# One accumulator bank per block product, and a scale vector spread by the matrix engine, in a fused attention and feed-forward kernel

## The chip, the core and the metric

The kernel runs on one core of a Trainium2 chip. A core has a matrix engine (TensorE, PE in the profile, with its weight loads listed as PEld), VectorE (DVE), ScalarE (ACT), GpSimd (POOL), a sync engine that here only issues transfers (SP), and 16 DMA engines. The engines run their own instruction streams and meet at semaphores. Matrix products land in PSUM, an accumulator memory made of banks; one tile of the pool `mm` below is one bank (128 partitions x 512 fp32). VectorE and ScalarE read PSUM and write the results back to SBUF.

The metric is the device time of one execution in microseconds (us), the median of several runs. The profile of one execution shows a span that is about 2 us shorter than that time.

## The reference

A chunked attention is followed by a feed-forward block with a residual.

```python
# q, k, v: (4, 8, 768, 64); mem_k, mem_v: (4, 8, 8, 64)
for c in range(24):                                   # chunks of 32 queries
    k_full = concat(mem_k, k[c*32-16 : c*32+40])      # 8 memory rows, 16 to the left, 8 to the right
    v_full = concat(mem_v, v[same])
    a = softmax(q_c @ k_full.T / sqrt(64))
    out[c] = a @ v_full
x  = out as (4, 768, 512)
mu, var = mean(x), mean((x - mu)**2)                  # over the last axis
xn = (x - mu) / sqrt(var + 1e-6) * g_ln               # g_ln: 512 numbers
y  = x + max(xn @ w_ch1, 0) @ w_ch2                   # 512 -> 2048 -> 512
```

## The kernel before

The rows are worked in 24 tiles of 128, three tiles to a stage, eight stages (`u` = 0 to 7). A stage has 28 steps: 16 steps of the first product (`up`, line 411), then the second product (`down`, line 441). From stage 2 on, two of the three tiles of the second product are computed together as a 2x2 block product with seven block multiplications in place of eight (a Winograd form): the left sums are `SA`, the right sums `T`, and each of the seven is a `product` (line 484) of eight matmuls of 128x256. They stand in steps 20 to 26, after `down` of the third tile.

```python
def product(p, left, right):                          # line 484
    for h in range(2):
        for k_ in range(4):
            nc.tensor.matmul(out=p, lhsT=left(h)[:, k_, :], rhs=right(h)[:, k_, :], ...)

def paired(u, n):                                     # n = 0 .. 6
    cols = [slice(0, 256), slice(256, 512)]
    # scaled(r, y, z, w): osb[r][:, w] = y * rstd[r] + z[r][:, w]   on VectorE (line 500)
    # minus(o, a, b, op): o = a op b                                on VectorE (line 458)
    for m in {0: (0,), 2: (2,), 3: (4, 3)}.get(n, ()):
        pair_slot[m] = slot("mm")                     # next of the four mm banks
    q = pair_slot
    if n == 0:
        product(q[0][:, cols[0]], a(0, 0), b(0, 0))
        nc.scalar.copy(out=three[:, 0, :], in_=q[0][:, cols[0]])       # line 524
    elif n == 1:
        product(q[0][:, cols[1]], part(SA, 1), part(T, 1))             # same bank as n == 0
        minus(psum, q[0][:, cols[1]], three[:, 0, :], ALU.add)
    elif n == 2:
        product(q[2][:, cols[0]], part(SA, 0), part(T, 0))
        minus(three[:, 2, :], q[2][:, cols[0]], psum, ALU.add)
        for h in range(2):
            mixed_r(h, 3)                             # the left sum that product 5 needs
        scaled(0, free(three, 0, [[512, 2], [1, 256]]), x)
    elif n == 3:
        product(q[3][:, cols[1]], part(SA, 2), part(T, 2))
        minus(three[:, 1, :], q[3][:, cols[1]], psum, ALU.add)
        scaled(1, free(three, 256, [[1, 512]]), x)
        if u == 7:
            scaled(1, q[3][:, cols[1]], o, cols[1])
            store(1, cols[1])
    elif n == 4:
        product(q[4][:, cols[0]], a(0, 1), b(1, 0))
    elif n == 5:
        product(q[4][:, cols[1]], part(SA, 1), b(1, 1))
        scaled(0, q[4], o)
        store(0)
    else:                                             # n == 6
        product(q[3][:, cols[0]], a(1, 1), part(T, 3))
        w = cols[0] if u == 7 else slice(0, 512)
        scaled(1, q[3][:, w], o, w)
        store(1, w)
```

The values of the eight memory rows are copied into the value buffers `V` by `v_mem`, 12 groups to a batch. For batches 2 and 3 ScalarE does this, in three copies of 8x2560 that the schedule puts in stages 1 and 3:

```python
for i in range(3):
    at(w - 1, (16, 19, 21)[i], v_mem, b, 4 * i, 4 * i + 4, act)   # w - 1 is stage 1, then stage 3
```

Ahead of the stages stands a start in which every step waits for its first data. The vector g_ln is read from memory 128 times, once for each partition, into `gb`, and used by `norm`. `warm(n)` are matmuls on zeros whose results nobody reads; they keep the matrix engine occupied.

```python
first_load(0, 0, 0, 32, nc.sync)                      # k of the first block
first_load(0, 1, 0, 32, nc.scalar)
nc.sync.dma_start(out=memkf, in_=...)                 # mem_k
first_load(1, 0, 0, 16, nc.sync)                      # q of the first block, in halves
first_load(1, 1, 0, 16, nc.gpsimd)
first_load(1, 0, 16, 32, nc.sync)
first_load(1, 1, 16, 32, nc.sync)
nc.sync.dma_start(out=xs[5][96:W, :], in_=...)        # mem_v of batch 0
nc.sync.dma_start(out=gb, in_=dram(moe_g_ln, 0, [[0, 128], [1, 512]]))
...                                                   # GpSimd queue: k, then V groups 0 and 1, w1, V 2 and 3, q, w1, ...
def norm(b, t):                                       # line 357
    i = NT * b + t
    nc.vector.scalar_tensor_tensor(
        out=xn[i % 4], in0=xs[i % 9], scalar=nmean[t], in1=gb, op0=ALU.add, op1=ALU.mult)
...
K0 = [as16(mm[0]), as16(mm[1])]
Q0 = [as16(mm[2]), as16(mm[3])]
...
scores(0, 0)
mem_vals()                                            # ScalarE: mem_v to fp16
soften(0, 0, 0)
soften(0, 0, 1)
mix(0, 1, 0, dve)
transpose_block(0, 1, 0, Q0)
v_mem(0, 0, 2, dve)
mix_raw(1, raws[1], None, dve, 64, 128)               # second half of q
warm(2, 512, att[1][:, 0, :])
half_q(0, 0, 1, as16(att[1][:, 1, :]))
first_right(0, 3, Q0)
part_q(0, 0, 1, as16(att[1][:, 1, :]), dve)
v_mem(0, 2, 4, dve)
values(0, 0)                                          # line 337: needs V groups 0 and 1
norm(0, 0)
window(0, 0, K0, 2, act)
window(0, 0, K0, 3, act)
warm(2, 512, att[0][:, 1, :])
scores(0, 1)
soften(0, 1, 0)
soften(0, 1, 1)
warm(4, 512, mm[1])
turn_x(0, 0)
values(0, 1)                                          # V groups 2 and 3
norm(0, 1)
...
late = up_tile(0, 0, 0, None)                         # first tile of stage 0; needs w1
```

Of the kernel before, what the change touches and what calls it, by code (L numbers as in the profile page):

```python
# [11 lines left out]
ALU = mybir.AluOpType  # L12
# [3 lines left out]
def kernel(  # L16
# [12 lines left out]
    nc = tc.nc  # L29
# [60 lines left out]
    def dram(t, offset, pattern):  # L90
        return bass.AP(tensor=t.tensor, offset=offset, ap=[list(p) for p in pattern])

    def free(ap, off, pattern, parts=None):
        p = list(ap.ap[0]) if parts is None else [ap.ap[0][0], parts]
        return bass.AP(tensor=ap.tensor, offset=ap.offset + off, ap=[p] + [list(x) for x in pattern])

    def as16(t):
        return t.bitcast(FP16)
# [104 lines left out]
    def first_right(b, g, banks):  # L203

        for half in range(2):
            copy(dve, free(KT[b % 2], GW * g + 80 + 4 * half, [[W, 4], [1, 4]]),
                 free(banks[half], 0, [[1, 4], [128, 4]]))
# [11 lines left out]
    def transpose_block(b, blk, which, banks):  # L219
        i = pick(iv, ("b", b, blk, which))  # L220
        for r in range(8):
            pv = banks[r // 4 if len(banks) == 2 else 0]
            c = 128 * (r % 4 if len(banks) == 2 else r)
            nc.tensor.matmul(  # L224
                out=pv[:, c : c + 128], lhsT=i[:, 128 * r : 128 * r + 128], rhs=identity,
                is_transpose=True, start=True, stop=True,
            )
# [26 lines left out]
    def part_q(b, blk, half, pv, eng):  # L254
        copy(eng, free(QR[b % 2], 1024 * blk + 64 * half, [[128, 8], [1, 64]]),
             free(pv, 64 * half, [[128, 8], [1, 64]]))

    def mix_raw(which, srcs, half, eng, lo=0, hi=128):

        o = pick(iv, ("b", 0, 0, which))[lo:hi, :]  # L260
        r0, n = (0, 8) if half is None else (4 * half, 4)
        for par in range(2):
            copy(eng, free(o, 128 * r0 + 64 * par, [[128, n], [1, 64]]),
                 free(srcs[par][lo:hi, :], 64 * r0, [[64, n], [1, 64]]))
# [87 lines left out]
            out=nmean[t], in0=tot[t], scalar1=-1.0 / 512, scalar2=None, op0=ALU.mult  # L352
        )

    def norm(b, t):
        i = NT * b + t
        nc.vector.scalar_tensor_tensor(  # L357
            out=xn[i % 4], in0=xs[i % 9], scalar=nmean[t], in1=gb, op0=ALU.add, op1=ALU.mult,
        )
# [97 lines left out]
    def minus(o, x, y, op=ALU.subtract):  # L457
        nc.vector.tensor_tensor(out=o, in0=x, in1=y, op=op)  # L458
# [22 lines left out]
    def product(p, left, right):  # L481
        for h in range(2):
            for k_ in range(4):
                nc.tensor.matmul(  # L484
                    out=p, lhsT=left(h)[:, k_, :], rhs=right(h)[:, k_, :],
                    start=(h == 0 and k_ == 0), stop=(h == 1 and k_ == 3),
                )
# [3 lines left out]
    def paired(u, n):  # L491

        t = 3 * u
        o = [osb[(t + r) % 3] for r in range(2)]
        x = [xs[(t + r) % 9] for r in range(2)]
        rs = [rstd[(t + r) % 9] for r in range(2)]
        cols = [slice(0, 256), slice(256, 512)]

        def scaled(r, y, z, w=slice(0, 512)):
            nc.vector.scalar_tensor_tensor(  # L500
                out=o[r][:, w], in0=y, scalar=rs[r], in1=z[r][:, w], op0=ALU.mult, op1=ALU.add,
            )

        def store(r, w=slice(0, 512)):
            i = t + r
            nc.sync.dma_start(
                out=out[i // 6, 128 * (i % 6) : 128 * (i % 6) + 128, w], in_=o[r][:, w]
            )

        def b(c, d):  # L510
            return lambda h: w2c[2 * c + h][:, :, cols[d]]

        def a(r, c):
            return lambda h: quarter(r, c, h)

        def part(lst, m):
            return lambda h: lst[m][h]

        for m in {0: (0,), 2: (2,), 3: (4, 3)}.get(n, ()):
            pair_slot[m] = slot("mm")  # L520
        q = pair_slot
        if n == 0:
            product(q[0][:, cols[0]], a(0, 0), b(0, 0))
            nc.scalar.copy(out=three[:, 0, :], in_=q[0][:, cols[0]])  # L524
        elif n == 1:
            product(q[0][:, cols[1]], part(SA, 1), part(T, 1))
            minus(psum, q[0][:, cols[1]], three[:, 0, :], ALU.add)
        elif n == 2:
            product(q[2][:, cols[0]], part(SA, 0), part(T, 0))
            minus(three[:, 2, :], q[2][:, cols[0]], psum, ALU.add)  # L530
            for h in range(2):
                mixed_r(h, 3)
            scaled(0, free(three, 0, [[512, 2], [1, 256]]), x)
        elif n == 3:
            product(q[3][:, cols[1]], part(SA, 2), part(T, 2))
            minus(three[:, 1, :], q[3][:, cols[1]], psum, ALU.add)
            scaled(1, free(three, 256, [[1, 512]]), x)
            if u == 7:
                scaled(1, q[3][:, cols[1]], o, cols[1])
                store(1, cols[1])  # L540
        elif n == 4:
            product(q[4][:, cols[0]], a(0, 1), b(1, 0))
        elif n == 5:
# [3 lines that stand above are left out]
        else:  # L547
# [5 lines that stand above are left out]
    def warm(n, m=512, p=None):  # L553
        p = mm[3] if p is None else p
        for _ in range(n):
            nc.tensor.matmul(out=p[:, 0:m], lhsT=zero[:, 0:128], rhs=zero[:, 0:m], start=True, stop=True)
# [4 lines left out]
    def first_load(which, par, lo, hi, eng):  # L561
        eng.dma_start(
            out=raws[which][par][4 * lo : 4 * hi, :],
            in_=dram((k, q)[which], 4 * par * HS + 512 * lo, [[512, hi - lo], [HS, 4], [1, 512]]),
        )
# [3 lines left out]
    nc.sync.dma_start(out=memkf, in_=dram(mem_k, 0, [[512, 32], [1, 512]]))  # L569
    first_load(1, 0, 0, 16, nc.sync)  # L570
    first_load(1, 1, 0, 16, nc.gpsimd)
    first_load(1, 0, 16, 32, nc.sync)
    first_load(1, 1, 16, 32, nc.sync)
    nc.sync.dma_start(out=xs[5][96:W, :], in_=dram(mem_v, 0, [[64, 8], [512, 8], [1, 64]]))
    nc.sync.dma_start(out=gb, in_=dram(moe_g_ln, 0, [[0, 128], [1, 512]]))

    def load_mem_v():
        nc.gpsimd.dma_start(
# [28 lines left out]
    nc.vector.memset(zero, 0.0)  # L607
    clear_keys(0, dve)
    nc.vector.memset(mhalf, -0.5)
    nc.vector.memset(memv16.bitcast(FP32)[96:W, :, :, 32:40], PAIR)  # L610
    total(band[:, 0:1], 56, 96)
    total(band[:, 1:2], 0, 32)
# [36 lines left out]

    K0 = [as16(mm[0]), as16(mm[1])]  # L650
    Q0 = [as16(mm[2]), as16(mm[3])]
    warm(10)
    mix_raw(0, raws[0], 0, dve)
    mix_raw(0, raws[0], 1, act)
# [15 lines left out]
    soften(0, 0, 0)  # L670
    soften(0, 0, 1)
    mix(0, 1, 0, dve)
    transpose_block(0, 1, 0, Q0)
    v_mem(0, 0, 2, dve)
    mix_raw(1, raws[1], None, dve, 64, 128)
    warm(2, 512, att[1][:, 0, :])
    half_q(0, 0, 1, as16(att[1][:, 1, :]))
    first_right(0, 3, Q0)
    part_q(0, 0, 1, as16(att[1][:, 1, :]), dve)
    v_mem(0, 2, 4, dve)  # L680
    values(0, 0)
    norm(0, 0)
    window(0, 0, K0, 2, act)
    window(0, 0, K0, 3, act)
    warm(2, 512, att[0][:, 1, :])
    scores(0, 1)
    soften(0, 1, 0)
    soften(0, 1, 1)
# [1 line left out]
    turn_x(0, 0)  # L690
    values(0, 1)
    norm(0, 1)
    window(0, 1, Q0, 0, act)
    window(0, 1, Q0, 1, act)
    key_left(0, 4, dve)
    turn["mm"] = 3
    late = up_tile(0, 0, 0, None)
# [2 lines left out]
    Q1 = as16(slot("mm"))  # L700
    half_q(0, 1, 0, Q1)
    part_q(0, 1, 0, Q1, act)
    window(0, 1, Q0, 2, dve)
    window(0, 1, Q0, 3, act)
    turn_x(0, 1)
    scores(0, 2)
    soften(0, 2, 0)
# [96 lines left out]
    for b in (2, 3):  # L804
        u = 2 * b - 1
        w = u - 1
        for blk in range(3):
            if b == 3 and blk == 0:
                at(w - 1, 0, pace, 0, 0)
            at(w - 1, 0 if b == 3 else 21, load_pair, b, blk)  # L810
        at(w, 0, mem_cols, b, pool)
        at(w - 1, 24, pace_x, 6 * b - 4)
        for g in range(NG):
            at(w - 1, 24 + g // 4, load_v, b, g)
        for i in range(3):
            at(w - 1, (16, 19, 21)[i], v_mem, b, 4 * i, 4 * i + 4, act)
        for blk in range(3):
            for which in range(2):
                at(w, (3, 9, 18)[blk] + which, mix, b, blk, which, dve)
                at(w, (7, 18, 23)[blk] + 3 * which, cross, b, blk, which)  # L820
        at(w, 18, spread, b, 0, dve, act)
        at(w, 27, spread, b, 1, dve, act)
        at(u, 9, spread, b, 2, dve, act)
        attend(6 * b, 2, 7, u)
        attend(6 * b + 1, 7, 13, u)
        attend(6 * b + 2, 13, 18, u)
# [61 lines left out]
```

## Time and profile before

| | |
|---|---|
| time, median of 3 runs | 223.66 us (223.60 to 223.71) |
| span of the profiled run | 221.6 us |
| PE busy | 209.3 us, 2116 matmuls |
| VectorE, ScalarE, GpSimd busy | 156.8, 124.7, 101.3 us |
| line 411 (`up`), 448 matmuls of 128x384 | 78.5 us |
| line 441 (`down`), 192 of 128x512 | 45.0 us |
| line 484 (`product`), 336 of 128x256 | six groups of 56 |
| ScalarE copies of memory values into V, 6 of 8x2560 | 13.8 us, 2320 ns each |

How to read it: the page gives for each engine its busy time, then the span in 40 slices of 5.54 us with the busy share in tenths, the granted clock of the matrix engine and what the DMA engines did. The chain of work that ended last follows the end of the span back to what released each step. The timeline gives each engine's instructions in order of time, with the idle time before them in brackets and who ended it. A letter q after an engine's name is its queue.

### The profile page before, as it was taken

The numbers are of one execution on the slowest core, as the hardware profiler recorded it, in microseconds if no ns is written. First come the engines' busy times: TensorE is split into PE (matmuls) and PEld (weight loads), VectorE is DVE, ScalarE is ACT, GpSimd is POOL, SyncE is SP. The second block draws the span as 40 slices with busy tenths as digits, with TensorE's granted clock in tenths as the row PEclk, the third lists the DMA queues.
The fourth block names the chain that finished last, engine by engine and source line by source line (L and its number), as shares of the span: only waits on it lengthen the run. The fifth ranks groups of instructions, "written<-read, shape, count | busy, mean of one in ns | idle before, by whom it ended". The sixth has DMA issues, their size and how long they took to land.

```text
span 221.6 us, 5419 instructions
## 1 busy us (share of the span) xinstructions
PE 209.3 (94%) x2116; PEld 142.7 (64%) x2116; DVE 156.8 (71%) x396; ACT 124.7 (56%) x242; POOL 101.3 (46%) x173
## 2 busy tenths in 40 slices
PE   7779999999999999999997999999999999999992
PEld 2437996557655566587655776586757675676571
DVE  5747467597969967985686678983888469563564
ACT  3735678418789768435899467427841576024100
POOL 7857589798998992407531983200111011100000
PEclk9967999999999999999999999999999999999999
DMA  6999999999979999697972999496312211220012
GB/s 167 172 194 191 199 198 188 196 148 241 161 103 152 184 194 120 110 189 159 196 121 74 91 186 130 96 165 144 26 24 71 98 24 28 71 95 3 0 47 95
DMA packets 72449, 27.98 MB, mean 126 GB/s; under 512 B 60392, under 2 KB 68328, under 8 KB 72424
## 3 DMA queue, kind: packets, MB, share of 16 engines
q0 software_dynamic: 46112, 14.71, 62.4%
q1 hardware_dynamic: 26168, 12.67, 27.2%
q10 hardware_dynamic: 144, 0.26, 0.5%
q8 instruction: 16, 0.26, 0.5%
q14 instruction: 9, 0.07, 0.1%
HBM read 30.54 MB, written 6.29 MB: 166 GB/s over the span
## 4 chain that ended last, share of the span: by engine, by line
PE 74%; ACT 4%; DVE 2%; issue 1%; ACTq 0%
PE mm L411 34%; PE mm L441 16%; PE mm L484 16%; PE att L316 5%; PE att L337 3%; ACT V L102 2%; DVE osb L500 1%; ACT three L524 1%; PE att L224 1%; PE mm L224 1%; ACT junk L362 0%; ACT AT L326 0%; PE att L385 0%; DVE SA L458 0%; DVE three L458 0%
## 5 line engine op out<-in xcount | busy, mean ns | idle before, releaser
L411 PE MATMUL mm<-xT,w1c 128*128 128x384 f16 x448 | 78.5, 328 | 0.0
L411 PEld LDWEIGHTS <-w1c 128*128 128x128 f16 x448 | 49.1, 114 | 21.0
L403 ACT ACTIVATE rT<-mm 128x384 f16<-128x384 f32 (+1 forms) x76 | 37.9, 502 | 37.5 <-PE mm L411 33.2
L405 DVE TENSOR_SCALAR rT<-mm 128x384 f16<-128x384 f32 (+1 forms) x48 | 27.3, 568 | 26.1 <-PE mm L411 25.6
L441 PE MATMUL mm<-w2c,rT 128*128 128x512 f16 x192 | 45.0, 380 | 0.0
L128 POOL DMA_DIRECT2D V<-in_v_dram x48 | 37.8, 795 | 6.8 <-DMA V<-in_v_dram 2.9
L326 ACT ACTIVATE AT<-att,band 104x512 f16<-104x512 f32 x48 | 31.3, 685 | 12.4 <-PE att L316 11.9
L368 POOL TENSOR_SCALAR veps<-sq 128x1 f32<-128x1 f32 x24 | 7.6, 318 | 64.3 <-ACT junk L362 56.2
L441 PEld LDWEIGHTS <-rT 128*128 128x128 f16 x192 | 17.7, 98 | 18.7
L484 PEld LDWEIGHTS <-SA 128*128 128x128 f16 x192 | 18.8, 98 | 6.9 <-issue 4.8
L362 ACT ACTIVATE junk<-xs,nmean 128x512 f16<-128x512 f32 x24 | 17.4, 725 | 9.1 <-DVE nmean L351 6.9
L484 PE MATMUL mm<-T,SA 128*128 128x256 f16 x144 | 16.7, 272 | 3.7 <-ACT three L524 3.7
L357 DVE SCALAR_TENSOR_TENSOR xn<-xs,nmean,gb 128x512 f16<-128x512 f32 x24 | 17.9, 747 | 0.3
L345 DVE SCALAR_TENSOR_TENSOR xs<-att,rec 128x512 f32<-128x512 f32 x24 | 16.6, 692 | 0.8
L372 POOL TENSOR_TENSOR rstd<-veps,mhalf 128x1 f32<-128x1 f32 x24 | 15.8, 658 | 2.0
L484 PEld LDWEIGHTS <-rT 128*128 128x128 f16 x144 | 14.1, 98 | 4.0 <-issue 1.0
L316 PE MATMUL att<-QR,KT 64*104 64x64 f16 x384 | 15.8, 234 | 0.7 <-ACT QR L102 0.6
L316 PEld LDWEIGHTS <-KT 64*104 64x104 f16 x384 | 12.6, 132 | 5.3 <-issue 3.7
L120 POOL DMA_DIRECT2D st<-in_k_dram x22 | 13.8, 662 | 1.8 <-DMA w1c<-in_moe_w_ch_dram 1.4
L337 PEld LDWEIGHTS <-AT 104*64 104x64 f16 x384 | 8.5, 114 | 8.5 <-issue 2.9
L102 ACT COPY V<-memv 8x2560 f16<-8x2560 f16 x6 | 13.8, 2320 | 0.1
L120 POOL DMA_DIRECT2D st<-in_q_dram x20 | 12.1, 650 | 1.2 <-DMA w2c<-in_moe_w_ch_dram 0.5
(92 smaller groups left out, 252.3 us busy)
## 6 DMA issues: line engine op xcount, KB each, us to landing
out_dram<-osb SPq DMA_DIRECT2D x23, 256.0 KB, 2.2
V<-in_v_dram POOLq DMA_DIRECT2D x40, 96.0 KB, 6.1
st<-in_k_dram POOLq DMA_DIRECT2D x22, 128.0 KB, 5.9
st<-in_q_dram POOLq DMA_DIRECT2D x20, 128.0 KB, 6.0
w1c<-in_moe_w_ch_dram POOLq DMA_DIRECT2D x4, 512.0 KB, 9.4
w2c<-in_moe_w_ch_dram POOLq DMA_DIRECT2D x4, 512.0 KB, 8.2
V<-in_v_dram POOLq DMA_DIRECT2D x8, 80.0 KB, 6.6
xT<-xn SPq DMA_TRANSPOSE x17, 3.1
```

The source lines that it names most:

```text
L102: eng.copy(out=out, in_=in_)
L120: nc.gpsimd.dma_start(out=s[:, 512 * par : 512 * par + 512], in_=dram((k, q)[which], (b * H + 4 * par) * HS + blk * 256 * D, [[512, 32], [ ...
L128: nc.gpsimd.dma_start(out=V[b % 2][lo:hi, g, :, 0:64], in_=dram(v, b * H * HS + (64 * g - 16 + lo) * D, [[64, hi - lo], [HS, H], [1, 64]]),)
L316: nc.tensor.matmul(out=p[0:W, par, (4 * gg + j) * 64 : (4 * gg + j) * 64 + 64], lhsT=KT[b % 2][rows, 2 * t + gg, j, :], rhs=free(QR[b % 2] ...
L326: nc.scalar.activation(out=free(AT[t % 3], 32 * c, [[64, 16], [1, 32]]), in_=free(p, 4 * c, [[64, 16], [1, 4], [8, 8]], W), func=ACTF.Exp, ...
L357: nc.vector.scalar_tensor_tensor(out=xn[i % 4], in0=xs[i % 9], scalar=nmean[t], in1=gb, op0=ALU.add, op1=ALU.mult,)
L362: nc.scalar.activation(out=junk, in_=xs[(NT * b + t) % 9], func=ACTF.Square, bias=nmean[t], scale=1.0, accum_out=sq[t],)
L403: nc.scalar.activation(out=o, in_=p, func=ACTF.Relu)
L405: nc.vector.tensor_scalar(out=o, in0=p, scalar1=0.0, scalar2=None, op0=ALU.max)
L411: nc.tensor.matmul(out=p, lhsT=free(w1c[c][:, dt, :], i, [[4, 128]]), rhs=xT[u % 2][:, dt, 128 * lo : 128 * (lo + n)], start=(dt == 0), st ...
L441: nc.tensor.matmul(out=p, lhsT=rT[c][:, k_, 128 * i : 128 * i + 128], rhs=w2c[c][:, k_, :], start=(c == 0 and k_ == 0), stop=(c == 3 and k ...
L484: nc.tensor.matmul(out=p, lhsT=left(h)[:, k_, :], rhs=right(h)[:, k_, :], start=(h == 0 and k_ == 0), stop=(h == 1 and k_ == 3),)
```

## The change

It has four parts.

1. In the paired block products, the second product goes to a bank of its own (`q[1]`), and the third takes the free half of the first product's bank. The number of banks in use is the same. The addition `scaled(0, three)` moves from step n = 2 to the end of n = 3. It is meant to let the second product start without the copy of the first.
2. The ScalarE copies of memory rows into V move from steps 16, 19 and 21 to steps 17, 21 and 24, to keep them off the copy of the first product.
3. g_ln is loaded once, as one row into a tile of zeros, and spread to all 128 rows by a product with a matrix of ones (fp32, two halves of 128x256, on the matrix engine). The first `norm` reads the result in PSUM; ScalarE copies it to `gb` for the later ones. Two pairs of `warm` go away.
4. In the start, mem_v is loaded ahead of the second half of q, the keys of block 1 are transposed into one bank (`K1`) in place of two, so that bank `mm[3]` is free for g, and VectorE's instructions stand in another order.

```diff
-    def norm(b, t):
+    def norm(b, t, gb=gb):
@@ paired
-        for m in {0: (0,), 2: (2,), 3: (4, 3)}.get(n, ()):
+        for m in {0: (0,), 1: (1,), 3: (4, 3)}.get(n, ()):
             pair_slot[m] = slot("mm")
@@
-            product(q[0][:, cols[1]], part(SA, 1), part(T, 1))
-            minus(psum, q[0][:, cols[1]], three[:, 0, :], ALU.add)
+            product(q[1][:, cols[0]], part(SA, 1), part(T, 1))
+            minus(psum, q[1][:, cols[0]], three[:, 0, :], ALU.add)
         elif n == 2:
-            product(q[2][:, cols[0]], part(SA, 0), part(T, 0))
-            minus(three[:, 2, :], q[2][:, cols[0]], psum, ALU.add)
+            product(q[0][:, cols[1]], part(SA, 0), part(T, 0))
+            minus(three[:, 2, :], q[0][:, cols[1]], psum, ALU.add)
             for h in range(2):
                 mixed_r(h, 3)
-            scaled(0, free(three, 0, [[512, 2], [1, 256]]), x)
@@ n == 3, after scaled(1, ...) and the store of u == 7
+            scaled(0, free(three, 0, [[512, 2], [1, 256]]), x)
@@ first loads
+    nc.sync.dma_start(out=xs[5][96:W, :], in_=dram(mem_v, 0, [[64, 8], [512, 8], [1, 64]]))
     first_load(1, 0, 16, 32, nc.sync)
     first_load(1, 1, 16, 32, nc.sync)
-    nc.sync.dma_start(out=xs[5][96:W, :], in_=dram(mem_v, 0, [[64, 8], [512, 8], [1, 64]]))
-    nc.sync.dma_start(out=gb, in_=dram(moe_g_ln, 0, [[0, 128], [1, 512]]))
@@ after the first memsets
+    gpad, gone = xs[7], xs[8][:, 0:128]
+    nc.vector.memset(gpad, 0.0)
+    nc.vector.memset(gone, 1.0)
+    nc.sync.dma_start(out=gpad[0:1, :], in_=dram(moe_g_ln, 0, [[512, 1], [1, 512]]))
@@ the start
+    K1 = [as16(mm[2])[:, 512 * h : 512 * h + 512] for h in range(2)]
+    def spread_g(half):
+        cols = slice(256 * half, 256 * half + 256)
+        nc.tensor.matmul(out=mm[3][:, cols], lhsT=gone, rhs=gpad[:, cols], start=True, stop=True)
@@
-    transpose_block(0, 1, 0, Q0)
+    transpose_block(0, 1, 0, K1)
+    mix_raw(1, raws[1], None, dve, 64, 128)
+    spread_g(0)
+    half_q(0, 0, 1, as16(att[1][:, 1, :]))
     v_mem(0, 0, 2, dve)
-    mix_raw(1, raws[1], None, dve, 64, 128)
-    warm(2, 512, att[1][:, 0, :])
-    half_q(0, 0, 1, as16(att[1][:, 1, :]))
-    first_right(0, 3, Q0)
     part_q(0, 0, 1, as16(att[1][:, 1, :]), dve)
+    first_right(0, 3, K1)
+    values(0, 0)
+    spread_g(1)
+    norm(0, 0, mm[3])
     v_mem(0, 2, 4, dve)
-    values(0, 0)
-    norm(0, 0)
     window(0, 0, K0, 2, act)
     window(0, 0, K0, 3, act)
-    warm(2, 512, att[0][:, 1, :])
+    copy(act, gb, mm[3])
     scores(0, 1)
@@ later windows of block 1: Q0 becomes K1
@@ the schedule
-            at(w - 1, (16, 19, 21)[i], v_mem, b, 4 * i, 4 * i + 4, act)
+            at(w - 1, (17, 21, 24)[i], v_mem, b, 4 * i, 4 * i + 4, act)
```

## The prediction

> **What bounds the kernel now.** I read the page first, then the chain in order of time, then the timelines of the places where the chain leaves the matrix engine, and last the start, which the chain does not reach (its first piece is at 41.13 us).
>
> ```profile
> PE 209.3 (94%) x2116; PEld 142.7 (64%) x2116; DVE 156.8 (71%) x396; ACT 124.7 (56%) x242; POOL 101.3 (46%) x173
> ...
> PE   7779999999999999999997999999999999999992
> ...
> PEclk9967999999999999999999999999999999999999
> DMA  6999999999979999697972999496312211220012
> ```
>
> PE is busy 94% of the span, and after the third slice (16.6 us) no slice but one and the last falls below nine tenths. So work on another engine is hidden, and time can be won in three places only: in PE's gaps, in the start, and behind PE's last product. The clock row shows more: two slices, from 11 to 22 us, ran at 0.6 and 0.7 of the full clock.
>
> The gaps are in the chain. One is plain, and one is longer (columns: start, length, what):
>
> ```profile
> 93.32 0.89 PE mm L484 x8
> 94.20 0.02 issue
> 94.23 0.38 ACT three L524
> 94.61 0.04 issue
> 94.65 5.40 PE mm L484 x48
> ...
> 114.47 4.55 ACT V L102 x2
> 119.03 0.01 issue
> 119.04 0.38 ACT three L524
> ```
>
> The first product of a pair (8 matmuls, 0.89 us) ends at 94.20, ScalarE copies it (0.38 us), and the other 48 matmuls start at 94.65. The list of waits has this as PE waiting for line 524: 3.7 us in six times, the longest 1.4. The long one is stage 3: the product ends at 117.06 + 0.89 = 117.95, but the copy stands behind two copies of memory rows on ScalarE (4.55 us) and starts at 119.04.
>
> At the end of the span the chain leaves PE again:
>
> ```profile
> 215.53 0.35 DVE three L458
> ...
> 215.90 0.76 DVE osb L500
> 216.66 0.02 issue
> 216.69 0.50 DVE osb L500
> 217.19 0.04 issue
> 217.23 1.05 PE mm L484 x8
> ```
>
> The seventh product waits until VectorE has read the other half of its bank, 0.87 us after the sixth product's last matmul.
>
> For the start, the PE timeline from 4 to 14 us and the transfer list:
>
> ```profile
> 12.17 0.19 PE L337 MATMUL att<-V,AT 104*64 104x65 f16 x1 [0.91 <-DMA V<-in_v_dram]
> 12.61 0.60 PE L337 MATMUL att<-V,AT 104*64 104x65 f16 x15 [0.26 <-DMA V<-in_v_dram]
> ...
> gb<-in_moe_g_ln_dram SPq DMA_DIRECT2D x1, 256.0 KB, 7.2
> ```
>
> The first `values` waits for V groups 0 and 1, issued at 4.20 and 4.98 us and landed at about 12.0 and 12.6. The load of `gb`, 256 KB issued at 4.79, lands at 12.0 as well: it shares the DMA engines with V all that time.
>
> **What the Trainium skill says.** "PSUM — Partial Sum Buffer", section "PSUM bank collisions raise a hardware error", says that two engines must be kept apart on a bank even at different columns. The trace agrees: the second product's columns are its own, and still it starts only 0.04 us after the copy of the other columns. "TensorE: Matmul & The Clock Gate", "Part 1: The HAM clock gate", says that the clock halves after an idle window of about 3.4 us, that the windows run freely, and that a busy one restores it. The trace shows 0.50 from about 12.35 to 19.07 us, 6.72 us, after a stretch (8.90 to 12.35) in which PE was busy 1.90 of 3.45 us. "DMA: Bandwidth & Descriptors", "Queues, rings and completion order", says that a DMA engine takes turns between the queues, which fits `gb` and V landing together. "FP8 and Floating Point Precision", "TensorE Precision Notes", gives four passes for true fp32; the trace before has no fp32 matmul.
>
> **Part 1 and 2, the gaps of stages 2 to 6.** With a bank of its own the second product needs only its left sums, which VectorE finished long before (stage 2: at 92.8 us, product at 94.2). The third needs the copy of the first, which has the 0.87 us of the second product to hide in and takes 0.38. In stage 3 only one memory copy (2.32 us) is now ahead of it: 114.47 + 2.32 = 116.79, before the product's end at 117.95. The two later ones run to about 123.9, just as ScalarE gets its first work of stage 4. So all five gaps close: 0.44 (stage 2), 119.47 - 117.95 = 1.52 (stage 3), 0.45, 0.44, 0.44: **3.3 us**. Products 5 and 6 need VectorE's sums and `three`: product 6 would start near 98.6 instead of 99.01 in stage 2, and with `scaled(0)` moved back the last sum is out near 97.6. No new wait there.
>
> **Part 1, stage 7.** The second product starts at 211.38 instead of 211.83. VectorE, with the spacings of the trace before: `psum` 212.50, third sum 213.33, left sums 213.67, then `three` at 214.34 (it was 215.45), `scaled(1)` 214.79, the half of bank q3 0.79 later at 215.58, done at 216.08. The seventh product starts near 216.12 instead of 217.23. But VectorE now has `scaled(0)` still to do: 215.99, then 216.78 for q4, and 217.44 for the last half, done at 217.92 instead of 218.78. The last store follows a store issued at about 217.55 that holds the queue some 0.65 (between the two earlier issues, 217.20 and 217.87), so it goes out near 218.2, not 218.82: **0.6 us**.
>
> **Part 3 and 4, the start.** Removed: 128 rows of 2 KB. The ScalarE queue moved 0.26 MB in 144 packets for 0.5% of the span, that is 1.1 us of all 16 engines; `gb` should have cost about the same, 1.0 us. V then lands near 11.1 and 11.6. Everything else for the first `values` is there by then: VectorE turns the second half of q by 10.0 (two casts of 0.50 and 0.41 after 9.1), memory rows by 10.5, PE's half transposes by about 10.7. Added on PE: two fp32 products, an estimate from the four passes and from 0.109 us per 128x256 matmul (0.87 / 8): 0.44 us each, 0.87 at half clock. They take the place of two pairs of `warm` (0.60 and 1.03 us), so PE's work is about the same. Added on VectorE: memsets of some 0.5 and 0.15 us in an idle time of 0.85 (1.76 to 2.61). Added on ScalarE: one copy of about 0.6 us while it waits for PE (idle 3.57 before 15.06). The first `values` ends near 12.1, before at 13.21: 1.1 us. What comes after depends on the clock. If it is halved as before from 12.3 on, the fp32 product and `warm(4)` are slow, and of the 1.1 only some 0.7 is left when the clock is back (19.1). If it stays full, the work from 12.35 to 19.07 shrinks and the next limit is DMA again: V groups 2 and 3 (landed 15.9 and 16.4, now a microsecond earlier) for the second `values`, which was at 17.19, and a key block at 28.5 with its transposes at 30.16; so the win ends near 2.0. PE is busier in the deciding stretch, but not by much, so I put the start at **1.3 us**, between 0.7 and 2.0. PE runs without a gap from there on, so it is kept.
>
> Sum: 3.3 + 0.6 + 1.3 = 5.2. 223.66 - 5.2 = **218.4 us**.
>
> **Rivals.** (a) *The start gives nothing*: V's time to land is set by its own packets (the GpSimd queue has 46112 packets and 62.4% of the engines' span), `gb` only filled holes; or the single row of g arrives late, since it is queued last, and PE, which works in order, waits in front of the half transposes. For it: mem_v, issued at 4.22, took until 8.79, and the margin to 9.8 us is one microsecond. Against it: V waits while `gb` is moving. Then 223.66 - 3.9 = 219.8. (b) *The gap returns elsewhere*: the third product waits for the copy when ScalarE is late, or the seventh for VectorE. For it: the stage 7 chain. Against it: ScalarE is idle before five of the six copies. It would give back up to 0.44 in each of six stages, 221 at the worst. (c) *The clock stays full through the start*: start 2.0 to 2.8, 217 to 217.7. For it: the first `values`, one fp32 product and part of `scores` now fall ahead of 12.3 us. Against it: from 12.35 to 15.70 PE was busy 3.09 of 3.35 us and the clock still stayed at 0.50, so more is needed than being busy.
>
> **Range and chances.** The gaps are nearly certain (3.3, at least 2.8), the tail 0.3 to 0.9, the start 0 to 2.8. 216.7 to 220.2 should hold it 8 times in 10. Two per cent is 4.47 us, 219.19: that asks for more than 0.57 of the start when the rest is as said. Faster by over 2%: 0.74; within 2%: 0.25; slower: 0.01.
>
> **What would show it.** In the changed profile PE's wait for line 524 should be gone and a pair's seven products stand 0.87 us apart; line 524 in stage 3 should start 0.03 us after its product; the first `values` should run near 11.6; the seventh product of stage 7 should start 1.1 us earlier relative to the first, the last VectorE instruction 0.9. The clock row shows which of (a) and (c) holds. I am wrong if PE waits for g, if `values` is still at 12.2, or if the third product waits for ScalarE.

## The result and the profile after

The changed kernel takes 216.74 us (median of 4 runs, 216.61 to 218.15), the kernel before in the same session 223.69. The ratio is 0.9696, with a 95% interval of 0.9655 to 0.9736. The prediction was 218.4 with a range from 216.7 to 220.2, so the time lies in the range, by 0.04 us at its lower end. The win is 6.95 us, forecast 5.2.

The page of the changed kernel, the rows that answer to those shown of before:

```profile
PE 205.8 (95%) x2116; PEld 141.1 (65%) x2116; DVE 159.3 (74%) x398; ACT 125.2 (58%) x243; POOL 101.5 (47%) x173
...
PE   7769998999999999999999999999999999999992
...
PEclk9999999999999999999999999999999999999999
DMA  6999999999979999999992599997212211220012
```

PE's busy time fell by 3.5 us with the same 2116 matmuls: the two slices of 0.6 and 0.7 in the clock row are gone. The low slice of PE in the middle is gone too; that was stage 3. In the chain in order of time, the seven products are now one piece, in stage 2 and in stage 3:

```profile
92.85 6.11 PE mm L484 x56
...
116.14 6.11 PE mm L484 x56
```

The PE timelines show how tight that is (start, length). First stages 2 and 3 of the kernel before:

```profile
93.15 1.04 PE L484 MATMUL mm<-w2c,rT 128*128 128x256 f16 x8
94.65 2.78 PE L484 MATMUL mm<-T,SA 128*128 128x256 f16 x24 [0.46 <-ACT three L524]
...
117.06 1.04 PE L484 MATMUL mm<-w2c,rT 128*128 128x256 f16 x8
119.47 2.78 PE L484 MATMUL mm<-T,SA 128*128 128x256 f16 x24 [1.37 <-ACT three L524]
```

And stage 3 of the changed kernel:

```profile
115.97 1.04 PE L484 MATMUL mm<-w2c,rT 128*128 128x256 f16 x8
116.85 2.78 PE L484 MATMUL mm<-T,SA 128*128 128x256 f16 x24
119.47 1.04 PE L484 MATMUL mm<-w2c,rT 128*128 128x256 f16 x8
```

From the first product's start to the second's are 0.88 us; before it was 94.65 - 93.15 = 1.50 in a plain gap and 119.47 - 117.06 = 2.41 in stage 3. From the first product to the stage after, a plain pair took 6.73 to 6.74 us and takes 6.11 to 6.12; stage 3 took 7.64 and takes 6.12. That is 4 x 0.62 + 1.52 = 4.0 us.

At the end (timeline, stage 7), the seventh product still waits for VectorE, but 0.20 and not 0.87 us:

```profile
210.19 1.04 PE L484 MATMUL mm<-w2c,SA 128*128 128x256 f16 x8
...
211.43 1.03 PE L484 MATMUL mm<-T,rT 128*128 128x256 f16 x8 [0.20 <-DVE osb L500]
```

From the first product of stage 7 to the end of the span it was 221.6 - 210.29 = 11.31 us and is 216.4 - 205.82 = 10.58: 0.73.

In the start, the PE timeline of the changed kernel reads:

```profile
11.59 0.44 PE L337 MATMUL att<-V,AT 104*64 104x65 f16 x16 [0.60 <-ACT KT L102]
11.96 0.70 PE L659 MATMUL mm<-xs,xs 128*128 128x256 f32 x2
12.59 0.65 PE L316 MATMUL att<-QR,KT 64*104 64x64 f16 x16
13.17 1.04 PE L556 MATMUL mm<-zero 128*128 128x512 f16 x4
14.13 0.40 PE L385 MATMUL att<-identity,xn 128*128 128x128 f16 x4
15.92 0.44 PE L337 MATMUL att<-V,AT 104*64 104x65 f16 x16 [1.39 <-ACT AT L326]
```

V groups 0 and 1, issued at the same times as before, land 5.0 and 5.6 us after their issue in place of 7.8 and 7.6, at about 9.2 and 10.6. The first `values` no longer waits for them; it runs in one piece, 0.44 us instead of 0.60 for 15 of its matmuls. What releases it is VectorE's copy of the half transposes out of the same PSUM tile, which ends at 11.48. (The bracket names ScalarE; the runs e1 and e5 below, with the same wait, name VectorE's QR.) The first tile of `up` starts at 16.29, before at 17.77; the next group at 19.57, before at 21.50. So 1.9 us are won by 20 us. This execution, one of 218.15 us, then lost 1.6 of them: its first matmul of stage 1 is at 48.16 in the PE timeline, before at 48.53. PE waits 0.79 us at 34.14 for the queries of block 2, whose transfer took 8.0 to 9.6 us to land. The other profiles of the new start without an edit to it keep the win (46.39 to 46.98 in e3, e6, e8 and e10 below).

### The profile page after: what moved, and what is told of

Its sections match the earlier page's. It is cut to its first block, busy times and chain, and to the rows that moved or that the text cites. A ratio compares the mean times of both kernels' runs of the same rounds, so it can differ in the third digit from the quotient of the medians.

```text
span 216.4 us, 5415 instructions
## 1 busy us (share of the span) xinstructions
PE 205.8 (95%) x2116; PEld 141.1 (65%) x2116; DVE 159.3 (74%) x398; ACT 125.2 (58%) x243; POOL 101.5 (47%) x173
## 4 chain that ended last, share of the span: by engine, by line
PE 75%; DMA 17%; DVE 3%; POOL 2%; issue 1%; DVEq 0%; POOLq 0%
PE mm L411 35%; PE mm L441 15%; PE mm L484 15%; DMA w1c<-in_moe_w_ch_dram 8%; PE att L316 5%; DMA st<-in_k_dram 5%; DMA st<-in_q_dram 4%; PE att L337 3%; DVE osb L500 1%; POOL st L120 1%; POOL V L128 1%; PE att L224 1%; PE mm L224 1%; DVE three L458 0%; DVE iv L104 0%
## 5 line engine op out<-in xcount | busy, mean ns | idle before, releaser
L357 DVE SCALAR_TENSOR_TENSOR xn<-xs,nmean,gb 128x512 f16<-128x512 f32 x23 | 17.2, 747 | 0.5 <-DVE nmean L351 0.3
L372 POOL TENSOR_TENSOR rstd<-veps,mhalf 128x1 f32<-128x1 f32 x24 | 16.5, 686 | 2.0
L104 DVE COPY iv<-st 128x1024 f16<-128x1024 f16 (+1 forms) x22 | 11.1, 521 | 3.8 <-DMA st<-in_q_dram 2.0
```

What stands on the lines that cost most here:

```text
L357: nc.vector.scalar_tensor_tensor(out=xn[i % 4], in0=xs[i % 9], scalar=nmean[t], in1=gb, op0=ALU.add, op1=ALU.mult,)
L372: nc.gpsimd.tensor_tensor(out=rstd[(NT * b + t) % 9], in0=veps[t % 3], in1=mhalf, op=ALU.pow)
```

## The experiments

Each is the kernel before or the changed kernel with one edit. Ratios are to the kernel before on the same chip.

### e1: the bank alone

```diff
 kernel before
+ part 1 (bank of its own, scaled(0) after scaled(1))
  at(w - 1, (16, 19, 21)[i], v_mem, ...)      # as before
  start as before
```

> Kernel before with part 1 alone: bank of its own for the second product, and scaled(0) moved; memory copies on ScalarE stay at steps 16, 19, 21, start as before. My theory: each plain gap is worth 0.62 us start to start (first product at 93.15, second at 94.65, 0.875 of that is work), four of them 2.5; in stage 3 the third product now waits for the late copy (it ends near 119.4, the third product could start near 118.8), so only 0.9 of 1.5 there; end of stage 7 0.7. Sum 4.1: 219.6 us. Rival, that most of the win is in the start: under 2 us, so over 221.6.

Measured: 219.45 us, ratio 0.9817 (0.9774 to 0.9860). The plain gaps are gone, and stage 3 has the smaller wait that was expected, on the third product (PE timeline):

```profile
116.21 1.04 PE L484 MATMUL mm<-w2c,rT 128*128 128x256 f16 x8
117.08 1.04 PE L484 MATMUL mm<-T,SA 128*128 128x256 f16 x8
118.62 1.58 PE L484 MATMUL mm<-T,SA 128*128 128x256 f16 x13 [0.50 <-ACT three L524]
```

Of stage 3's gap of 1.52 us, 0.66 are left: the third product starts 118.62 - 117.08 = 1.54 us after the second instead of 0.88.

### e2: the bank and the later copies

```diff
 e1
-            at(w - 1, (16, 19, 21)[i], v_mem, ...)
+            at(w - 1, (17, 21, 24)[i], v_mem, ...)
```

> Kernel before with parts 1 and 2, start as before. My theory: stage 3 gives its whole 1.53, the sum is 4 x 0.62 + 1.53 + 0.7 = 4.7: 218.9 us, 0.6 to 0.7 below the run with part 1 alone, and PE has no wait for line 524 nor for the copies. Rival, that the later copies push other ScalarE work of stages 1 and 4 back: the same time as part 1 alone, 219.6, with waits of PE for ScalarE in stage 4.

Measured: 219.0 us, ratio 0.9783 (0.9746 to 0.9819). PE has no wait for line 524 at all, and no wait for ScalarE in stage 4. The step from e1 is 0.45 us by the medians, within the intervals; the 0.66 is shown by the traces alone. Together, parts 1 and 2 are worth 223.58 - 219.0 = 4.6 us, as the trace of the changed kernel says (4.0 + 0.7).

### e3: the start alone

```diff
 changed kernel
- part 1, part 2
```

> Changed kernel with parts 1 and 2 undone: only the start differs from the kernel before. My theory: 1.9 to 2.2 us are won by 24 us and 1.5 to 2.0 reach the end: 221.5 to 222.1 us, clock full from 5.5 us on, six waits for line 524 of 3.7 us in all as before. Rival, that transfers between 24 and 48 us take the win back, as in the profile of the changed kernel, where PE waits 0.79 us at 34.14 and only 0.4 is left at 48 us: 223.2 us.

Measured: 221.61 us, ratio 0.9916 (0.9887 to 0.9945): 2.0 us. In its profile stage 1 starts at 46.98 us, before at 48.53, so the win is not lost between 24 and 48 us. The wait for line 524 is back (3.7 us, six times). 4.6 and 2.0 make 6.6; the whole change made 6.95 on its chip, and 6.4 in e10. So the two halves add up.

### e4: more zero matmuls

```diff
 kernel before
-    warm(2, 512, att[1][:, 0, :])
+    warm(5, 512, att[1][:, 0, :])
     half_q(0, 0, 1, ...)
+    warm(4, 512, att[1][:, 0, :])
```

> Kernel before with the zero matmuls between 9.6 and 12.1 us raised from 2 to 5 and 4 more after the half transposes: the load of g for 128 rows stays, so V still lands at 12.0 and 12.6. It tells clock from transfers. If the clock is what was won: it stays full after 12.35 us, and the first half of stage 0 shrinks by 1 us or more: 222.3 to 222.8. If the earlier landing of V is what counts: under 0.4 won, 223.3 to 223.7, even with a full clock.

Measured: 223.9 us, ratio 1.001 (0.9991 to 1.003). In its profile the clock is full from 12.35 to 19.07 us, and its mean over the span is 0.997 in twelve runs, against 0.990 of the kernel before on that chip. So nothing was won. But its profile shows that the edit itself held the start. PE waited for the first half of q, the clock was 0.50 from 8.1 to 11.5 us, and the half transposes came at 12.51, before at 10.85. The four matmuls added behind them write the tile that VectorE's copy of them reads, so this copy waited until 13.91 and the first `values` until 14.44, long after V had landed:

```profile
13.91 0.42 DVE L104 COPY QR<-att 128x512 f16<-128x512 f16 x1 [2.21 <-PE att L556]
```

At full clock PE then made up for it: the first tile of `up` is at 17.82 against 17.77, the next group at 21.01 against 21.50. Stage 1 nevertheless starts at 49.66, before at 48.53. So this run doesn't tell the clock from the transfer, as it was meant to; it shows only that this way to a higher clock wins nothing.

### e5: the transfer of g put back

```diff
 changed kernel
     nc.sync.dma_start(out=gpad[0:1, :], ...)
+    nc.sync.dma_start(out=T[3][1] as fp32, in_=dram(moe_g_ln, 0, [[0, 128], [1, 512]]))   # read by nobody
```

> Changed kernel, with the old transfer of g to 128 rows issued as well, right after the one row, into a tile that nobody reads yet. It puts the 256 KB back on the DMA engines and leaves all else as in the changed kernel. If the transfer is what held V: V groups 0 and 1 land near 12.0 and 12.6 again instead of 9.2 and 10.6, the first values starts near 12.2 instead of 11.6, and 0.6 to 1.5 us are lost: 217.3 to 218.2. If V is set by its own packets: it lands as in the changed kernel and the time stays at 216.7.

Measured: 218.98 us, ratio 0.9803 (0.9773 to 0.9833). V groups 0 and 1 take 8.0 and 8.3 us again, and the first `values` waits for the second of them (PE timeline):

```profile
12.47 0.19 PE L337 MATMUL att<-V,AT 104*64 104x65 f16 x1 [0.56 <-DVE QR L104]
13.31 0.41 PE L337 MATMUL att<-V,AT 104*64 104x65 f16 x15 [0.65 <-DMA V<-in_v_dram]
```

That is the time of e2 (219.0), with the new start in place. One transfer of 256 KB that nobody waits for takes back the whole win of the start, more than the 0.6 to 1.5 us expected.

V is not all of it in this profile. The first half of q is cast from 7.69 us on, in the changed kernel from 6.50, and the half transposes are 0.92 us later (11.51 against 10.59); then come the 0.65 us of waiting for V. And the clock fell: it is 0.50 from 14.4 to 17.8 us, and its mean over the span is 0.987 to 0.990 in all four runs, in the changed kernel 0.995 or more. How the loss divides between these is not shown, nor whether the transfer is what delayed q in this execution.

### e6: the addition in its old place

```diff
 changed kernel
         elif n == 2: ...
+            scaled(0, free(three, 0, [[512, 2], [1, 256]]), x)
         elif n == 3: ...
-            scaled(0, free(three, 0, [[512, 2], [1, 256]]), x)
```

> Changed kernel with scaled(0) back at step n = 2, the bank of its own kept. My theory: only stage 7 feels it. The last sum is 0.67 later on VectorE, so the seventh product starts 0.6 to 0.7 later, but VectorE has less to do after it; 0.2 to 0.4 us lost: 217.0. Rival, that VectorE holds the seventh product in every stage: up to 0.3 in each of six stages, 218.5.

Measured: 217.25 us, ratio 0.9724 (0.9685 to 0.9762). Only stage 7 has a wait for VectorE, so the rival is out:

```profile
210.33 1.03 PE L484 MATMUL mm<-T,rT 128*128 128x256 f16 x8 [0.87 <-DVE osb L500]
```

The seventh product starts 210.33 - 204.06 = 6.27 us after the first, in the changed kernel 211.43 - 205.82 = 5.61. VectorE's last instruction ends 7.83 us after the first product against 7.46. But the end of the span comes 10.64 us after it against 10.58. Moving the addition takes 0.66 us from PE's wait and is worth 0.06 us at the end in the traces, which no timing here resolves.

### e7: mem_v after q

```diff
 changed kernel
-    nc.sync.dma_start(out=xs[5][96:W, :], in_=...)     # ahead of the second half of q
     first_load(1, 0, 16, 32, nc.sync)
     first_load(1, 1, 16, 32, nc.sync)
+    nc.sync.dma_start(out=xs[5][96:W, :], in_=...)
```

> Changed kernel with mem_v loaded after the second half of q, as before. My theory: mem_v then lands near 8.8 and the row of g last; VectorE casts the second half of q first in any case, and the first values hangs on the half transposes (11.5), so nothing moves: 216.7, within 0.2. Rival, that the first memory copy becomes the last to come: first values up to 0.5 later, 217.2.

Measured: 217.52 us, ratio 0.9738 (0.9708 to 0.9767). The first `values` is at 11.79, in the changed kernel at 11.59 and in e10 at 11.71. The ratio's interval covers most of that of e10, so whether the order of these two loads is worth a few tenths stays open.

### e8: the copies in their old steps, with the bank

```diff
 changed kernel
-            at(w - 1, (17, 21, 24)[i], v_mem, ...)
+            at(w - 1, (16, 19, 21)[i], v_mem, ...)
```

> Changed kernel with the memory copies back at steps 16, 19, 21. As the third product, not the second, now waits for the ScalarE copy, the stage 3 loss should be 0.6 us and not 1.5: 217.3. Rival, that moving the copies is worth nothing once the bank is split: 216.7.

Measured: 217.72 us, ratio 0.9741 (0.9715 to 0.9768). The third product of stage 3 waits 0.49 us for the copy and starts 116.91 - 115.38 = 1.53 after the second, 0.65 more than without the wait, as in e1. Part 2 is worth that, by two traces; the ratios, 0.0025 above that of e10, agree but don't separate it.

### e9: the kernel before without g

```diff
 kernel before
-    nc.sync.dma_start(out=gb, in_=dram(moe_g_ln, 0, [[0, 128], [1, 512]]))
+    nc.vector.memset(gb, 1.0)          # the scale by g is left out
```

> Kernel before without the transfer of g: gb is filled with ones by VectorE in its idle time, so the scale by g is left out of the computation; the order of all else, the zero matmuls and the two-bank keys stay. It tells the 256 KB from the new order and from the fp32 products. If the transfer is the whole of the start's win: V lands near 9.2 and 10.6, the first values starts near 11.7 (its memory rows and transposes), and 1.7 to 2.1 us are won, as with all of the new start: 221.5 to 222. If the new order or the busier PE matter as well: 0.6 to 1.3 us, 222.3 to 223.

Measured: 221.44 us, ratio 0.9903 (0.9875 to 0.9931): 2.1 us, as much as the whole new start (2.0). But its profiled run is one of 223.18 us and shows what is behind the spread. V landed 5.2 and 4.9 us after issue, as in the changed kernel, and still the first `values` runs at 12.56, because the old order makes VectorE do the memory rows ahead of the second half of q; and the clock fell. The first view is the stretch from 12.35 to 19.07 us: its length, the busy time of PE, PEld, DVE, ACT and POOL, the granted clock (0.52), the busy share of the DMA engines and GB/s. The second is the PE timeline:

```profile
12.35:19.07 6.72, 6.51 (x73) 4.21 (x74) 3.86 (x12) 2.94 (x7) 3.66 (x7) 0.52 1.52 193
```

```profile
12.56 0.65 PE L337 MATMUL att<-V,AT 104*64 104x65 f16 x16 [0.56 <-issue]
13.15 1.03 PE L556 MATMUL att<-zero 128*128 128x512 f16 x2
...
17.78 1.55 PE L423 MATMUL mm<-xT,w1c 128*128 128x128 f16 x16
```

From 13.15 to 17.78 this is, to 0.01 us, the timeline of before, where the same matmuls stood at 13.15 and 17.77. The runs of this kernel sort themselves by the mean granted clock of the span:

| kernel, same chip | time by mean clock |
|---|---|
| e9 | 220.83 and 221.16 at 1.000; 221.33 and 221.54 at 0.992; 222.41 at 0.989; 223.18 at 0.982 |
| before | 222.85 at 1.000; five runs at 0.988 to 0.996: 223.19 to 224.02; five at 0.981 to 0.985: 223.39 to 224.37 |

With V early, the runs spread over 2.3 us, in the order of the clock; with V late, the middle of the low-clock runs (223.79) is hardly 1 us above the one run at 1.000. The run with V early and the lowest clock won next to nothing (223.18, in the midst of the runs of before), though in it VectorE's order held the first `values` as well. It looks as if the two are needed together. That is a pattern in six and eleven runs, not an experiment that sets the clock.

### e10: the changed kernel again

> The changed kernel itself once more, as the measure for the runs on this chip: 216.6 to 217.2 us. The win of 2 us in the start should be there by 24 us, and be cut in some executions by waits for transfers between 24 and 48 us.

Measured: 217.1 us, ratio 0.9716 (0.9692 to 0.9741); mean clock 0.9987 in six runs, none below 0.996. On this chip the kernel before took 223.5, with a mean clock of 0.988.

### e11: the exponentials ahead of the copy of g

```diff
 changed kernel
-    copy(act, gb, mm[3])
     scores(0, 1)
     soften(0, 1, 0)
     soften(0, 1, 1)
+    copy(act, gb, mm[3])
```

> Changed kernel with the ScalarE copy of g out of PSUM moved behind the two exponentials of the second tile. In the changed kernel that copy waits until norm has read the same bank (14.11) and holds the exponentials back, which could run at 13.3; PE waits 1.39 us for them. My theory: the second values then hangs on V groups 2 and 3 (landed 14.9 and 15.5) and starts 0.4 us earlier, and the half queries on their load (16.3): 0.2 to 0.4 us won, 216.4. Rival, that the whole 1.3 us is won: 215.5. Rival, that transfers between 24 and 48 us take all of it: 216.7.

Measured: 217.0 us, ratio 0.9702 (0.9671 to 0.9733), not to be told from e10; a sixth run of 219.13 us, over 1.5% above the fastest (215.73), is left out of both as a slow one. The wait that it removes is real. In the changed kernel the ScalarE timeline has

```profile
14.11 0.59 ACT L102 COPY gb<-mm 128x512 f32<-128x512 f32 x1 [2.40 <-DVE xn L357]
14.59 1.27 ACT L326 ACTIVATE AT<-att,band 104x512 f16<-104x512 f32 x2
```

with the scores done at 13.2: the copy waits for `norm`, which reads the same bank, and the exponentials wait behind the copy. In the profile of e11 PE's waits for line 326 are 0.2 us in all instead of 1.6, and the first tile of `up` is at 16.30, where the changed kernel has it too; but in that run the clock was 0.50 from 8.0 to 11.4 us and the first `values` late (12.78), so that this says little by itself. e12 has the same edit at full clock.

### e12: the loads in another order

```diff
 e11
-    load_w1(3)
     load_block(0, 2, 0)
+    load_w1(3)
     nc.gpsimd.memset(...)
+    load_w2(0)
+    load_block(0, 2, 1)
     load_v(0, 6)
     load_v(0, 7)
-    load_w2(0)
-    load_block(0, 2, 1)
+    load_w2(1)
     load_v(0, 8)
     load_v(0, 9)
-    load_w2(1)
     load_v(0, 10)
     load_v(0, 11)
-    at(0, 22, mix, 1, 0, 0, dve)
+    at(0, 24, mix, 1, 0, 0, dve)
```

> As the run before, and the loads in the GpSimd queue in another order: the keys of block 2 ahead of the fourth part of w1, the first part of w2 and the queries of block 2 ahead of V groups 6 and 7, the second part of w2 ahead of V 8 and 9; and VectorE's turn of the first key block of batch 1 two steps later, so that it doesn't hold up the transposed rows of tile 5 while it waits for its load. If transfers between 24 and 48 us limit the changed kernel: PE's waits of 0.8 and 0.3 us there go, and 0.5 to 1.5 us are won: 215.4 to 216.2. If V groups 6 to 9 now come too late, or the queue only shifts the wait: 216.5 or more.

Measured: 217.26 us, ratio 0.9717 (0.9690 to 0.9744): no gain over e10. Its PE timeline shows where the win of e11's edit goes in this execution:

```profile
15.78 1.08 PE L423 MATMUL mm<-xT,w1c 128*128 128x128 f16 x16
16.70 0.59 PE L556 MATMUL mm<-zero 128*128 128x512 f16 x2
18.77 0.40 PE L286 MATMUL mm<-identity,iv 64*128 64x64 f16 x8 [1.47 <-ACT iv L102]
```

The first tile of `up` is 0.6 us earlier than in e10 (16.41), and then PE waits 1.47 us for a half of q that ScalarE waited 1.75 us for from memory. (This half took 9.0 us to land here, 6.1 in e10 and 6.3 in e11.) From the second group of `up` to stage 1 it takes 47.46 - 20.43 = 27.0 us, in e10 46.97 - 19.68 = 27.3, in the first profile of the changed kernel 48.16 - 19.57 = 28.6. With the new order PE hardly waits there, but in e10 it didn't either, so against that profile there were 0.3 us to win. No version here beats the changed kernel.

## Why the prediction was right, and where it was not

**Gaps of stages 2 to 6, 3.3 us: right in kind, 4.0 in size.** The mechanism (second product held by the copy of the first, through the bank) is shown by e1 and e3. The term that was mis-sized is the plain gap, 0.44 each: it was read as the idle time between the pieces of the chain. In the PE timeline of before, stage 2, the first product starts at 93.15 and its copy at 94.23, 1.08 us later, where eight matmuls back to back take 0.875. These 0.2 us until the product is there to be copied are paid only where something waits for it, and they were not counted. With the copy (0.38) and the 0.04 after it they make 1.50 from start to start, so a gap costs 1.50 - 0.875 = 0.62. Stage 3, which was read from starts, came out as said (1.52).

**Stage 7, 0.6: right, for a partly wrong reason.** 0.73 measured. The seventh product starts 5.61 us after the first, before 217.23 - 210.29 = 6.94: 1.33 earlier, where 1.1 was forecast. But e6 shows that the moved addition has no part in the 0.73 that can be measured: with the addition in its old place the end still comes 0.67 earlier (10.64 against 11.31), and 0.67 is what the gap cost in stage 7 (1.54 from start to start before, 0.87 after).

**The start, 1.3: too small; 2.0 measured (e3).** Two terms failed.
- "`gb` should have cost about the same, 1.0 us": V landed 2.8 and 2.0 us earlier, and 8.0 and 8.3 us after issue again when the 256 KB were put back (e5). In all nine profiles without this transfer they take 4.7 to 6.2 us, in all five with it 7.6 to 8.3. The engine time of the transfer's own packets, 1.0 us, was the wrong measure for how long others wait because of it. The first `values` could use only part of it, since VectorE's copy took over as the last wait at 11.48, close to the 11.6 foreseen.
- "PE is busier in the deciding stretch, but not by much": from 8.90 to 12.35 us PE is busy 2.79 us of 3.45, before 1.90, and the clock stays at 1.00 from 12.35 to 19.07, as the prediction's third rival had it. The mean clock of the span is 0.995 or more in all eleven runs of the changed kernel. But how busy PE must be is not shown. In e5 the clock fell at 14.4 us after 3.4 us (11.03 to 14.44) with PE busy 2.20, and the changed kernel has a stretch as idle (2.02 from 12.60 to 16.01) at full clock. The Trainium skill's page "TensorE: Matmul & The Clock Gate", in "Part 1: The HAM clock gate", calls the windows free-running, so that where they fall would matter; that fits seven profiles with stretches at half clock, each 3.4 or 6.8 us long, which begin anywhere from 8.0 to 14.4 us, and the runs of before, whose mean clock varies between 0.981 and 1.000 without a change in the program.

All three terms came out above the forecast: 4.0 + 0.7 + 2.0 = 6.7 against 5.2. That the time still lies in the range, by 0.04 us, is luck in part; e10, on another chip, is at 217.1.

The rival that the start gives nothing is out: V did not land by its own packets alone (e5, e9). Nor is the win one of the new order or of the fp32 products: without them, taking the transfer away wins 2.1 us (e9), and with them, putting it back loses the win (e5). PE did not wait for the row of g. The rival that the gap returns elsewhere is out in the changed kernel, and would have been true of stage 3 without part 2, by 0.65 us (e1, e8). The fp32 products took 0.59 and 0.63 us from start to next start, not 0.44; they lay where zero matmuls had been.

What stays open: by which path the transfer costs the 2.0 us, and how they divide between late data and a low clock. The profiles say one thing about it. Three with the old start had more clock from 12.35 to 19.07 us than the profile of before (0.75 in e1 and e2, 1.00 in e4, against 0.50), and in them the second group of `up` starts earlier, at 20.81, 20.70 and 21.01, before at 21.50. But stage 1 starts at 48.40, 49.14 and 49.66, before at 48.53. With the new start e3 and e10 are at 19.70 and 19.68, and stage 1 at 46.98 and 46.97. So in these profiles what the clock gave while the data were late was all but gone by stage 1 (0.13 us in e1, nothing in the others). What early data give at a low clock is seen in one run only (e9), and no run set the clock by itself.

## What to carry to other kernels

Read what a gap costs from the start of one group to the start of the next, in the trace of the engine that waits, not from the idle time between two pieces of a chain. A transfer that spreads one row to all partitions moves as many bytes as a full tile (256 KB here); where the first data are awaited, load the row once and spread it on an engine that has time. And a load that nobody is seen waiting for can still be what delays the one that is waited for: put it back alone to see.

## What the runs showed of the hardware that was not expected

- One 256 KB transfer of 128 rows from one source row, issued beside the first loads, delayed two transfers in another queue by 2 to 3 us (4.7 to 6.2 us to landing in the nine profiles without it, 7.6 to 8.3 in the five with it).
- More clock in the start brought PE to the second group of `up` 0.5 to 0.8 us earlier in three profiles with late data (e1, e2, e4), but to stage 1 only 0.13 us earlier in one and 0.6 to 1.1 later in the others.
- The matrix engine's clock fell to one half for 3.4 or 6.8 us in seven of the fourteen profiles. By the mean clocks it did so in some runs of one kernel and not in others (before: 0.981 to 1.000).
- An fp32 product of 128x256 appears as two weight loads (0.19 us each) and two matmuls of 0.38 to 0.48 us, and occupies PE for about 0.6 us, where one fp16 matmul of that size takes 0.875 / 8 = 0.11.
